# An adaLN attention block on one core: a new order for the first tasks, and the first 1/std replicated before the last scale group's products

## The chip, the cores and the metric

The kernel runs on one core of one Trainium2 chip. The metric is the device time of one execution in microseconds (us), the median over several runs. The profiled execution is one more run with the hardware profiler on; its span goes from the first to the last instruction of the program, and its own device time is a little longer than the span.

The engines: PE is TensorE (PEld its weight loads), DVE is VectorE, ACT is ScalarE, POOL is GpSimd, SP is SyncE, which here only issues transfers. Each works through its instructions in order.

## The reference

Two batches of 256 tokens, width D = 1152, all bf16:

```
mod = (silu(c) @ w_mod).reshape(B, 6, 1, D)
shift_a, scale_a, gate_a, ... = mod[:, 0], mod[:, 1], mod[:, 2], ...
h   = layernorm(x) * (1 + scale_a) + shift_a
qkv = h @ wqkv
p   = softmax(q @ k.T * D**-0.5)
out = x + gate_a * ((p @ v) @ wo)
```

## The kernel before

**Tiling.** The 512 tokens are four tiles of 128 (0 and 1 are batch 0, 2 and 3 batch 1). D is nine chunks of 128, called `cc` or `k`. Everything up to the attention is held transposed, with features on the partitions and tokens along the free axis, so `x` is transposed on PE first.

**The layer norm is split.** The mean is subtracted from the transposed x (`center`, L375). The chunk is then multiplied by `1 + scale` (`scale_x`, L470), which gives `h0T_sb`, stored in the tile `pvT_sb`. The division by the standard deviation is not done there. It is applied later, where scores and v leave PSUM, and for that 1/std and std are needed in two layouts: one value per token on the partitions (`rstd_sb`), and replicated over all partitions along the tokens (`rep_sb`, `std_sb`). `rep(b)` (L410) makes the second layout for batch b with two f32 transposes on PE from `lnv_sb`, the logarithm of the variance; `rep_out(b)` (L417) turns them into `rep_sb` and `std_sb` with two exponentials on ACT. `std_sb` is first read by `shift_x` (L482).

**The loads.** SP issues every weight load in the order of the list `LOADS`, into tiles written for the first time, so no load waits for compute. In it lie, among others, the four groups of scale columns of `w_mod` (`s` 0 to 3, covering chunks 0-1, 2-3, 4-5 and 6-8), between the row blocks of the key weights (`w`). Group 3 is issued after key rows 4-5 and before rows 6, 7 and 8.

**The front, an order written out by hand.** The list `ORDER` (L169 to L181) gives the order in which tasks of the first stage are emitted. Since each engine is in order, it fixes the order on each engine. The tasks:

- `('cT',)`, `('cTo',)`, `('e1',)`, `('d1',)`, `('rc',)`, `('scT',)`: c is transposed on PE, copied out by ACT, and silu(c) is made from it over ACT, POOL, DVE and POOL again.
- `('warm', 4)`: four products of zeros on PE, after five others (`warm(WARM)`).
- `('sum', i)`: row sums of x tile i on ACT (L387); `('nmT', i)` (L361) transposes and replicates such a mean into PSUM bank 6 on PE; `('mean', 3)` (L390) makes the mean of tile 3 with nine products by a matrix of ones.
- `('xT', i, part)` (L345): four or five PE transposes of x tile i into a PSUM bank; `('out', i, part, engine)` (L352) copies them to `xnT_sb`.
- `('nm', b, engine)` (L366) copies the replicated means of batch b from PSUM to `nm_sb`; `('cen', cc, tiles, engine)` centres a chunk, `('scale', cc, tiles, engine)` scales it.
- `('smm', g)` (L440) multiplies silu(c) by scale group g on PE, in bank 7, and `('sev', g)` (L447) reads the result on DVE and adds 1.
- `('early', k, ...)` and `('late', k)` are the key products of chunk k for the first five and the last two of seven key columns, each accumulating in its own bank (L491).
- `('sq', i)` (L397) makes the sum of squares on ACT.

**Behind the list** the code continues with the variance of batch 0 (`rstd_c(0)`, L405 and L407), centring and scaling of group 2, two more sums of squares, and then a loop over groups 2 and 3 (L585) that emits the key products of chunks 4 to 8. In chunk 5, after three of the seven columns, it emits `s_mm(3)` (L435), `scale_group(3)` and `rstd_c(1)`, and then goes on with the other four columns of chunk 5. `rep(0)` and `rep_out(0)` stand behind chunk 6, `rep(1)` and `rep_out(1)` behind chunk 7.

Then follow on PE: two more key columns, the shift products (`h_mm`), the query columns, v, scores, the gate, p @ v, and the product with `wo`. The dependence tracker (`_Prog`) turns reads and writes into semaphore waits; for a PSUM bank every access of another engine is waited for, whatever the columns.

Of the kernel before, what the change touches and what calls it, by code (L numbers as in the profile page):

```python
# [21 lines left out]
class _Prog:  # L22
# [12 lines left out]
    def op(self, eng, fn, r=(), w=(), dma=False, extra=()):  # L35
        o = _Op()
        o.eng, o.fn, o.dma = eng, fn, dma
        o.sem = o.val = None
        o.inc = False
        deps = set(extra)  # L40
        for k in r:
            if k[0] == "ps":
                continue
            p = self.last_w.get(k)
            if p is not None and not (p.eng == eng == PE):
                deps.add(p)
            self.readers.setdefault(k, []).append(o)
        for k in w:
            if k[0] == "ps":
                continue  # L50
            for q in self.readers.get(k, ()):
                if q is not o and (q.dma or dma or q.eng != eng):
                    deps.add(q)
            p = self.last_w.get(k)
            if p is not None and p is not o and not (p.eng == eng == PE):
                deps.add(p)
            self.readers[k] = [o] if k in r else []
            self.last_w[k] = o
        for k in set(r) | set(w):
            if k[0] != "ps":  # L60
                continue
            accesses = self.bank.setdefault(k, {})
            for e, q in accesses.items():
                if e != eng:
                    deps.add(q)
            accesses[eng] = o
        deps.discard(o)
        o.deps = deps
        self.ops.append(o)
        return o  # L70
# [73 lines left out]
D = 1152  # L144
# [21 lines left out]
CENTRED = (0, 1)  # L166
CUT = ("w", "qa", 8)
WARM = 5
ORDER = [  # L169
    ('sum', 2), ('cT',), ('xT', 2, 0), ('warm', 4), ('nmT', 2), ('cTo',), ('e1',), ('sum', 0), ('xT', 3, 0),  # L170
    ('xT', 3, 1), ('d1',), ('out', 3, 1, 'A'), ('out', 2, 0, 'D'), ('rc',), ('nmu2',), ('sum', 1), ('xT', 1, 0),
    ('xT', 2, 1), ('scT',), ('xT', 0, 0), ('out', 3, 0, 'D'), ('out', 1, 0, 'D'), ('mean', 3),
    ('out', 2, 1, 'D'), ('out', 0, 0, 'D'), ('xT', 1, 1), ('out', 1, 1, 'A'), ('smm', 0), ('nm', 1, 'D'),
    ('nmT', 0), ('nmT', 1), ('cen', 0, (2, 3), 'D'), ('sev', 0), ('xT', 0, 1), ('cen', 0, (0, 1), 'D'),
    ('nm', 0, 'D'), ('scale', 0, (2, 3), 'A'), ('scale', 0, (0, 1), 'A'), ('out', 0, 1, 'A'),
    ('cen', 1, (0, 1, 2, 3), 'D'), ('scale', 1, (2, 3), 'D'), ('early', 0, (2, 3)), ('early', 0, (0, 1)),
    ('sum', 3), ('scale', 1, (0, 1), 'D'), ('cen', 3, (0, 1, 2, 3), 'D'), ('late', 0), ('sq', 0), ('late', 1),
    ('smm', 1), ('cen', 2, (0, 1, 2, 3), 'D'), ('sev', 1), ('early', 1), ('scale', 2, (2, 3), 'D'),
    ('scale', 2, (0, 1), 'D'), ('scale', 3, (2, 3), 'D'), ('scale', 3, (0, 1), 'D'), ('late', 2), ('late', 3),
    ('early', 2), ('sq', 1), ('smm', 2), ('early', 3),  # L180
]  # L181


def bass_standalone__dit_adaln_block__diffusion_kernel(
    nc: bass.Bass,
    x: bass.AP,
    c: bass.AP,
    wqkv: bass.AP,
    wo: bass.AP,
    w_mod: bass.AP,  # L190
    out: bass.AP,
):
    with ExitStack() as es:
        _build(nc, es, x, c, wqkv, wo, w_mod, out)


def _build(nc, es, x, c, wqkv, wo, w_mod, out):
# [117 lines left out]
    for k0 in range(0, DC, 3):  # L315
# [7 lines left out]
        out=ident[:, :], in_=ident[:, :], compare_op=ALU.not_equal, fill=1.0,  # L323
# [78 lines left out]
    def rstd_c(b):  # L402
        i0, i1 = 2 * b, 2 * b + 2
        two = [("sq", i0), ("sq", i0 + 1)]
        op(AC, lambda a: a.activation(lnv_sb[:, i0:i1], sq_sb[:, i0:i1], ACT.Ln, bias=eps_sb[:, 0:1], scale=1.0 / D),  # L405
           r=two + [("eps",)], w=[("lnv", i0), ("lnv", i0 + 1)])
        op(AC, lambda a: a.activation(rstd_sb[:, i0:i1], lnv_sb[:, i0:i1], ACT.Exp, scale=-0.5),  # L407
           r=[("lnv", i0), ("lnv", i0 + 1)], w=[("rstd", i0), ("rstd", i0 + 1)])

    def rep(b):  # L410
        for i in (2 * b, 2 * b + 1):
            lo = NTOK + (i % 2) * P
            src = bass.AP(lnv_sb, i, [[TT, P], [0, P]])
            op(PE, lambda pe, src=src, lo=lo: pe.transpose(ps[7][:, lo:lo + P], src, ident32[:, :]),  # L414
               r=[("lnv", i), ("ident32",)], w=[("ps", 7)])

    def rep_out(b):  # L417
        lo, hi = b * NTOK, (b + 1) * NTOK
        for dst, sc, key in ((rep_sb, -0.5, "rep"), (std_sb, 0.5, "std")):
            op(AC, lambda a, dst=dst, sc=sc: a.activation(dst[:, lo:hi], ps[7][:, NTOK:2 * NTOK], ACT.Exp, scale=sc),  # L420
               r=[("ps", 7)], w=[(key, b)])
# [18 lines left out]
    def s_mm(g):  # L440
        a, b_ = SGROUPS[g]
        if g < SROWS:
            mod_mm(s_ap(g), [("ws", g)], a, b_, 0, a)
        else:
            rows_mm(s_off[g], b_ - a, [("ws", g)], ("mr", 0, a))
# [42 lines left out]
    def qk_mm(tag, src, key, col, k, bank, tiles=(0, 1, 2, 3), start=None):  # L488
        lo, hi = tiles[0] * P, (tiles[-1] + 1) * P
        rk = [(key, k, i) for i in tiles] if key == "h0" else [(key, k, b) for b in range(B)]  # L490
        op(PE, lambda pe: pe.matmul(ps[bank][:, lo:hi], wq_sb[:, k, col * P:(col + 1) * P],  # L491
                                    src[:, k, lo:hi], start=(k == 0) if start is None else start,
                                    stop=(k == DC - 1), skip_group_check=True),
           r=[("w", tag, k)] + rk, w=[("ps", bank)])
# [17 lines left out]
    early, late = tuple(range(EARLY)), tuple(range(EARLY, NA))  # L512
# [58 lines left out]
    def scale_group(g):  # L571
        s_ev(g)
        a, b_ = SGROUPS[g]
        for cc in range(a, b_):
            for b in range(B):
                scale_x(cc, (2 * b, 2 * b + 1), AC if b == 1 else DVE)
        if g + 1 < len(SGROUPS):
            center_group(g + 1)
# [6 lines left out]
    for g in range(2, len(SGROUPS)):  # L585
        a, b_ = SGROUPS[g]
        for k in range(a, b_):
            for j in range(NA):
                qk_mm("ka", h0T_sb, "h0", DC + j, k, j)
                if j == 2 and k == b_ - 1 and g + 1 < len(SGROUPS):  # L590
                    s_mm(g + 1)
                    scale_group(g + 1)
                    if g == 2:
                        rstd_c(1)
            b = k - 6
            if b in CENTRED:
                rep(b)
                rep_out(b)
    def shift_group(g):
        a, b_ = HGROUPS[g]  # L600
        for n, (cc, b) in enumerate((cc, b) for cc in range(a, b_) for b in range(B)):
            shift_x(cc, b)
# [172 lines left out]
    for i in range(TT):  # L775
        b = i // 2
# [65 lines left out]
```

## Time and profile before

| | us |
|---|---|
| median of 5 runs | 98.18 (97.81 to 98.42) |
| profiled execution, own time | 98.14 |
| its span | 96.4 |
| PE busy | 90.2 (94%) |
| DVE busy | 51.1 (53%) |
| ACT busy | 32.1 (33%) |
| POOL busy | 2.0 (2%) |

The page cuts the span into 40 slices of 2.41 us. Matmuls are pipelined: a record begins when a matmul starts to stream and lasts until its modelled end, so consecutive records overlap, and the distance from start to start is what one costs PE. A few matmul records are missing from the trace (697 matmuls against 705 weight loads). In a timeline line stand the start, the length, the engine, the line of the kernel, the operation, the output, the inputs, the shape and the number of instructions merged into that line; in square brackets, the idle time before it and what ended it.

### The profile page before, as it was taken

What the parts mean: (1) busy time and instruction counts of PE and PEld (TensorE: products, weight loads), DVE (VectorE), ACT (ScalarE), POOL (GpSimd) and SP (SyncE); (2) the same over time, 40 slices, a digit from 0 to 9 for tenths busy, and PEclk for the clock granted to TensorE, in tenths of its full rate; (3) what the DMA queues carried; (4) which work ended last, traced back from release to release, by engine and by line L of the source; (5) the groups of instructions that cost most, each with busy time, mean ns of one, the idle gap of its engine ahead of it and who ended that gap; (6) DMA issues with size and microseconds to landing.
All of it is one profiled execution on the core that took longest, in us unless ns stands there. A gap on an engine that the chain in (4) does not pass through costs nothing.

```text
span 96.4 us, 1728 instructions
## 1 busy us (share of the span) xinstructions
PE 90.2 (94%) x697; PEld 50.4 (52%) x705; DVE 51.1 (53%) x131; ACT 32.1 (33%) x65; POOL 2.0 (2%) x12
## 2 busy tenths in 40 slices
PE   5995899979999999999999999999999999999990
PEld 1475555435545454444444487454448866555670
DVE  1155994840367739404612075554307747499971
ACT  2696996956542200003220203336025700000000
POOL 5020000000000000000000000000000000000000
PEclk9999999999999999999999999999999999999999
DMA  2999999999999999999999992211477575712222
GB/s 22 373 310 346 333 314 346 358 315 340 366 368 366 379 336 361 388 394 392 391 391 391 392 293 33 46 31 27 22 27 45 46 46 48 126 55 82 82 82 82
DMA packets 20667, 22.03 MB, mean 229 GB/s; under 512 B 2610, under 2 KB 16690, under 8 KB 20660
## 3 DMA queue, kind: packets, MB, share of 16 engines
q1 hardware_dynamic: 20512, 21.63, 77.6%
q10 hardware_dynamic: 148, 0.30, 0.9%
q8 instruction: 5, 0.08, 0.3%
q14 instruction: 2, 0.02, 0.0%
HBM read 19.76 MB, written 1.18 MB: 217 GB/s over the span
## 4 chain that ended last, share of the span: by engine, by line
PE 74%; SPq 10%; DMA 9%; issue 1%; ACT 1%; DVE 1%
PE psbank L491 27%; PE psbank L785 18%; PE psbank L669 16%; DMA wm_sb<-in_w_mod_dram 9%; SPq L291 7%; PE psbank L747 4%; PE psbank L685 4%; PE psbank L656 2%; SPq L284 1%; PE psbank L435 1%; SPq L280 1%; PE psbank L726 1%; ACT qkT_sb L340 1%; ACT pvT_sb L480 1%; PE psbank L414 0%
## 5 line engine op out<-in xcount | busy, mean ns | idle before, releaser
L491 PE MATMUL psbank<-pvT_sb,wq_sb 128*128 128x512 bf16 (+1 forms) x82 | 18.1, 366 | 0.9 <-ACT pvT_sb L480 0.4
L491 PE MATMUL psbank<-hT_sb,wq_sb 128*128 128x512 bf16 x79 | 17.5, 379 | 0.2 <-issue 0.2
L785 PE MATMUL psbank<-wm_sb,pvT_sb 128*128 128x384 bf16 x99 | 16.3, 326 | 0.0
L669 PE MATMUL psbank<-wq_sb,hT_sb 128*128 128x512 bf16 x70 | 15.6, 379 | 0.2 <-issue 0.2
L785 PEld LDWEIGHTS psbank<-wm_sb,pvT_sb 128*128 128x128 bf16 x99 | 9.7, 98 | 6.3
L491 PEld LDWEIGHTS psbank<-hT_sb,wq_sb 128*128 128x128 bf16 x81 | 7.9, 98 | 9.4
L491 PEld LDWEIGHTS psbank<-pvT_sb,wq_sb 128*128 128x128 bf16 x86 | 7.7, 97 | 8.8 <-ACT pvT_sb L480 1.3
L340 ACT ACTIVATE qkT_sb<-psbank 128x512 bf16<-128x512 f32 x9 | 4.9, 603 | 19.5 <-PE psbank L491 19.5
L669 PEld LDWEIGHTS psbank<-wq_sb,hT_sb 128*128 128x128 bf16 x72 | 6.9, 98 | 8.3 <-DVE nb_sb L700 0.2
L338 DVE CAST qkT_sb<-psbank 128x512 bf16<-128x512 f32 x9 | 5.7, 683 | 9.5 <-PE psbank L491 9.5
L798 DVE TENSOR_TENSOR ga_sb<-psbank,gate_rep 128x384 bf16<-128x384 f32 x11 | 6.1, 553 | 3.2 <-PE psbank L785 3.0
L679 DVE TENSOR_SCALAR v_sb<-psbank,rstd_sb 128x512 bf16<-128x512 f32 x4 | 3.0, 749 | 8.8 <-PE psbank L669 8.8
L484 DVE SCALAR_TENSOR_TENSOR hT_sb<-std_sb,sh_sb,pvT_sb 128x256 bf16<-128x256 f32 x18 | 7.3, 478 | 0.1
L382 DVE TENSOR_TENSOR xnT_sb<-xnT_sb,nm_sb 128x512 bf16<-128x512 bf16 (+1 forms) x9 | 5.6, 655 | 0.1
L677 ACT ACTIVATE v_sb<-psbank,rstd_sb 128x512 bf16<-128x512 f32 x4 | 2.7, 683 | 7.3 <-PE psbank L669 7.3
L398 ACT ACTIVATE junk_sb<-x_sb,nmu_sb 128x1152 bf16<-128x1152 bf16 x4 | 5.0, 1251 | 0.1
L387 ACT ACTIVATE junk_sb<-x_sb 128x1152 bf16<-128x1152 bf16 x4 | 4.6, 1157 | 0.8 <-DMA x_sb<-in_x_dram 0.8
L332 PE MATMUL psbank<-warm_sb 128*128 128x512 bf16 x9 | 3.7, 563 | 1.2 <-DVE warm_sb L319 1.2
L702 ACT ACTIVATE e_sb<-s_sb,nb_sb 128x256 bf16<-128x256 bf16 x4 | 2.0, 508 | 8.2 <-DVE nb_sb L700 8.2
L801 DVE TENSOR_TENSOR xo_sb<-x_sb,ga_sb 128x384 bf16<-128x384 bf16 x11 | 3.9, 358 | 0.4
L480 ACT ACTIVATE pvT_sb<-xnT_sb,s_sb 128x256 bf16<-128x256 bf16 x7 | 3.2, 501 | 2.7 <-DVE s_sb L456 2.6
L747 PE MATMUL psbank<-pT_sb,v_sb 128*128 128x256 bf16 x36 | 4.1, 272 | 0.0
(72 smaller groups left out, 72.8 us busy)
## 6 DMA issues: line engine op xcount, KB each, us to landing
wq_sb<-in_wqkv_dram SPq DMA_DIRECT2D x3, 864.0 KB, 11.0
wm_sb<-in_w_mod_dram SPq DMA_DIRECT2D x1, 2592.0 KB, 16.1
wm_sb<-in_wo_dram SPq DMA_DIRECT2D x1, 2592.0 KB, 21.8
wq_sb<-in_wqkv_dram SPq DMA_DIRECT2D x4, 448.0 KB, 8.3
wm_sb<-in_w_mod_dram SPq DMA_DIRECT2D x3, 576.0 KB, 7.5
wm_sb<-in_w_mod_dram SPq DMA_DIRECT2D x1, 1440.0 KB, 10.5
wq_sb<-in_wqkv_dram SPq DMA_DIRECT2D x6, 224.0 KB, 7.2
wq_sb<-in_wqkv_dram SPq DMA_DIRECT2D x2, 576.0 KB, 10.4
```

What stands on the lines that cost most here:

```text
L291: op(SP, lambda e: e.dma_start(wq_sb[:, k0:k1, c0:c1], wq_v[:, k0:k1, c0:c1]), w=[("w", tag, k) for k in range(k0, k1)], dma=True)
L338: op(DVE, lambda v: v.tensor_copy(dst, src), r=r, w=w)
L340: op(AC, lambda a: a.activation(dst, src, ACT.Copy), r=r, w=w)
L382: op(eng, lambda e: e.tensor_tensor(ap, ap, nm, ALU.add), r=[("xnT", cc, i) for i in tiles] + nk, w=[("xnT", cc, i) for i in tiles])
L387: op(AC, lambda a: a.activation(junk_sb[:, :], x_sb[:, i, :], ACT.Copy, scale=sc, accum_out=dst[:, i:i + 1]), r=[("x", i)], w=[("junk", 0) ...
L398: op(AC, lambda a: a.activation(junk_sb[:, :], x_sb[:, i, :], ACT.Square, bias=nmu_sb[:, i:i + 1], scale=1.0, accum_out=sq_sb[:, i:i + 1]) ...
L484: op(DVE, lambda v: v.scalar_tensor_tensor(hT_sb[:, cc, lo:hi], std_sb[:, lo:hi], sh_sb[:, cc, b:b + 1], h0T_sb[:, cc, lo:hi], op0=ALU.mul ...
L491: op(PE, lambda pe: pe.matmul(ps[bank][:, lo:hi], wq_sb[:, k, col * P:(col + 1) * P], src[:, k, lo:hi], start=(k == 0) if start is None el ...
L669: op(PE, lambda pe, k=k, c0=c0, c1=c1, bank=bank: pe.matmul(ps[bank][:, 0:c1 - c0], hT_sb[:, k, i * P:(i + 1) * P], wq_sb[:, k, 2 * D + c0 ...
L747: op(PE, lambda pe, h=h, cc=cc, sbk=sbk: pe.matmul(ps[bank][:, h * NTOK:(h + 1) * NTOK], v_sb[:, 2 * b + sbk, cc * P:(cc + 1) * P], pT_sb[ ...
L785: op(PE, lambda pe, i=i, k=k, rhs=rhs, n=n, bank=bank: pe.matmul(ps[bank][:, 0:n], pvT_sb[:, k, i * P:(i + 1) * P], rhs, start=(k == 0), s ...
L798: op(DVE, lambda v, b=b, c0=c0, c1=c1, n=n, bank=bank, s=s: v.tensor_tensor(ga_sb[:, s, 0:n], ps[bank][:, 0:n], gate_rep[:, b, c0:c1], ALU ...
```

## The change

Two edits. The list `ORDER` is written in another order, and some of its tasks go to another engine. The loop behind it emits `rep(0)` and `rep_out(0)` ahead of chunk 6 where it emitted them behind chunk 6; `rep(1)` stays behind chunk 7.

On PE the task list now has all transposes of x, `mean` of tile 3 and the three `nmT` ahead of `s_mm(0)`; before, `nmT(0)`, `nmT(1)` and five transposes of tile 0 came behind it. `cT` and the warm-up products now stand ahead of the first transposes of x. From `s_mm(0)` to chunk 3 the order on PE is the same. On ACT, the copy of c's transposes stands ahead of the first row sum, and both `nm` copies come to it from DVE. Of the scalings, chunk 0 goes from ACT to DVE, and the batch 1 halves of chunks 1 and 2 go from DVE to ACT. The copy-out `('out', 3, 1)` goes from ACT to DVE. The number of instructions of each kind is the same but for these moves. SP's list of loads is untouched.

```
 ORDER = [
-    ('sum', 2), ('cT',), ('xT', 2, 0), ('warm', 4), ('nmT', 2), ('cTo',), ('e1',), ('sum', 0), ('xT', 3, 0),
-    ('xT', 3, 1), ('d1',), ('out', 3, 1, 'A'), ('out', 2, 0, 'D'), ('rc',), ('nmu2',), ('sum', 1), ('xT', 1, 0),
-    ('xT', 2, 1), ('scT',), ('xT', 0, 0), ('out', 3, 0, 'D'), ('out', 1, 0, 'D'), ('mean', 3),
-    ('out', 2, 1, 'D'), ('out', 0, 0, 'D'), ('xT', 1, 1), ('out', 1, 1, 'A'), ('smm', 0), ('nm', 1, 'D'),
-    ('nmT', 0), ('nmT', 1), ('cen', 0, (2, 3), 'D'), ('sev', 0), ('xT', 0, 1), ('cen', 0, (0, 1), 'D'),
-    ('nm', 0, 'D'), ('scale', 0, (2, 3), 'A'), ('scale', 0, (0, 1), 'A'), ('out', 0, 1, 'A'),
-    ('cen', 1, (0, 1, 2, 3), 'D'), ('scale', 1, (2, 3), 'D'), ('early', 0, (2, 3)), ('early', 0, (0, 1)),
-    ('sum', 3), ('scale', 1, (0, 1), 'D'), ('cen', 3, (0, 1, 2, 3), 'D'), ('late', 0), ('sq', 0), ('late', 1),
-    ('smm', 1), ('cen', 2, (0, 1, 2, 3), 'D'), ('sev', 1), ('early', 1), ('scale', 2, (2, 3), 'D'),
-    ('scale', 2, (0, 1), 'D'), ('scale', 3, (2, 3), 'D'), ('scale', 3, (0, 1), 'D'), ('late', 2), ('late', 3),
-    ('early', 2), ('sq', 1), ('smm', 2), ('early', 3),
+    ('cT',), ('warm', 4), ('cTo',), ('sum', 2), ('nmT', 2), ('e1',), ('xT', 2, 0), ('d1',), ('xT', 0, 0),
+    ('xT', 3, 0), ('rc',), ('xT', 3, 1), ('xT', 2, 1), ('sum', 0), ('nmT', 0), ('out', 2, 0, 'D'), ('nmu2',),
+    ('out', 3, 0, 'D'), ('scT',), ('sum', 1), ('xT', 1, 0), ('out', 3, 1, 'D'), ('mean', 3), ('out', 0, 0, 'D'),
+    ('out', 2, 1, 'D'), ('nm', 1, 'A'), ('xT', 0, 1), ('xT', 1, 1), ('nmT', 1), ('out', 1, 0, 'D'),
+    ('out', 1, 1, 'A'), ('cen', 0, (2, 3), 'D'), ('smm', 0), ('cen', 0, (0, 1), 'D'), ('nm', 0, 'A'),
+    ('out', 0, 1, 'A'), ('sev', 0), ('scale', 0, (2, 3), 'D'), ('early', 0, (2, 3)), ('scale', 0, (0, 1), 'D'),
+    ('cen', 1, (0, 1, 2, 3), 'D'), ('scale', 1, (0, 1), 'D'), ('cen', 3, (0, 1, 2, 3), 'D'),
+    ('cen', 2, (0, 1, 2, 3), 'D'), ('early', 0, (0, 1)), ('late', 0), ('scale', 1, (2, 3), 'A'), ('late', 1),
+    ('smm', 1), ('sev', 1), ('sum', 3), ('scale', 2, (2, 3), 'A'), ('scale', 2, (0, 1), 'D'), ('early', 1),
+    ('sq', 0), ('scale', 3, (0, 1), 'D'), ('late', 2), ('sq', 1), ('scale', 3, (2, 3), 'D'), ('late', 3),
+    ('early', 2), ('smm', 2), ('early', 3),
 ]
```

```
     for g in range(2, len(SGROUPS)):
         a, b_ = SGROUPS[g]
         for k in range(a, b_):
+            if k == 6:
+                rep(0)
+                rep_out(0)
             for j in range(NA):
                 qk_mm("ka", h0T_sb, "h0", DC + j, k, j)
                 if j == 2 and k == b_ - 1 and g + 1 < len(SGROUPS):
                     s_mm(g + 1)
                     scale_group(g + 1)
                     if g == 2:
                         rstd_c(1)
-            b = k - 6
-            if b in CENTRED:
-                rep(b)
-                rep_out(b)
+            if k == 7:
+                rep(1)
+                rep_out(1)
+
     def shift_group(g):
```

## The prediction

> **What bounds the kernel now.** I read the page first, then the chain of waits, then the timeline of the first 25 us, because everything that the change touches lies there.
>
> ```profile
> PE 90.2 (94%) x697; PEld 50.4 (52%) x705; DVE 51.1 (53%) x131; ACT 32.1 (33%) x65; POOL 2.0 (2%) x12
> PE   5995899979999999999999999999999999999990
> PEclk9999999999999999999999999999999999999999
> DMA  2999999999999999999999992211477575712222
> ```
>
> PE is full from the tenth slice on; the holes are in the first nine (up to 21.7 us). The transfers are full until 58 us. So two bounds are possible early: PE's own front, or the loads. The chain in order of time says which:
>
> ```profile
> 8.36 2.54 SPq L291
> 10.90 0.04 issue
> 10.94 9.03 DMA wm_sb<-in_w_mod_dram
> 19.97 0.04 issue
> 20.01 0.59 PE psbank L435 x36
> 20.61 0.02 issue
> 20.63 0.29 DVE sh_sb L453
> 20.93 0.02 issue
> 20.95 0.17 DVE s_sb L456
> 21.12 0.02 issue
> 21.14 0.52 ACT pvT_sb L480
> 21.66 0.04 issue
> 21.71 1.69 PE psbank L491 x7
> 23.39 0.22 PE psbank L414 x2
> 23.61 1.51 PE psbank L491 x7
> ```
>
> The reader is to see three stretches. Until 19.97 the chain is the load queue alone: the last of the four scale groups lands there, and nothing computed before is on the chain. From 20.01 to 21.71 it is one round trip: scale products on PE, two steps on DVE, one scaling on ACT. From 21.71 it is PE without a hole worth naming, to 94.03 of 96.4. So a microsecond saved before 19.97 counts only if the load comes sooner too, and one saved on PE after 21.71 counts in full. The timeline around the landing gives the slack on both sides:
>
> ```profile
> 16.48 3.18 PE L491 MATMUL psbank<-pvT_sb,wq_sb 128*128 128x512 bf16 x14
> 20.01 0.57 PE L435 MATMUL psbank<-wm_sb,scT_sb 128*32 128x96 bf16 x36 [0.35 <-DMA wm_sb<-in_w_mod_dram]
> 20.51 0.55 PEld L491 LDWEIGHTS psbank<-pvT_sb,wq_sb 128*128 128x128 bf16 x4
> 20.74 0.81 PE L491 MATMUL psbank<-pvT_sb,wq_sb 128*128 128x512 bf16 x3 [0.16 <-DMA wq_sb<-in_wqkv_dram]
> 21.71 1.69 PE L491 MATMUL psbank<-pvT_sb,wq_sb 128*128 128x512 bf16 x7 [0.16 <-ACT pvT_sb L480]
> ```
>
> PE stood 0.35 us before the landing by modelled ends. A wide matmul occupies its slot for (1.69 - 0.38) / 6 = 0.218 us, where 0.38 is the length of a single record there; so the slot before had been free for about 0.35 + 0.38 - 0.22 = 0.5 us. That is PE's slack at the landing.
>
> **The change, part by part.**
>
> *rep(0) moved ahead of chunk 6.* Two f32 transposes leave the stream behind chunk 6: 0.22 us, from the chain (23.39 to 23.61), on the path. They come back behind the last four products of chunk 5. Four weight loads but three matmul records stand there, so one record is missing: the four start at 20.74 and every 0.213 to 0.218 us after it, and the last slot ends at about 21.60. Chunk 6 started at 21.71, when ACT's scaling (21.14 + 0.52 = 21.66) released it. The empty slot is 0.11 us. The transposes take it and 0.11 us more, so chunk 6 starts at 21.82 and ends 0.11 us later, but nothing of 0.22 us follows it. Sum: -0.22 + 0.11 = **-0.11 us**. Bounds: 0, if the gap is only the pipeline's drain and the transposes push chunk 6 by their whole 0.22; -0.22, if both fit, as by the modelled ends (20.74 + 0.81 = 21.55, then 0.16 idle) they nearly do. I take -0.11, from starts rather than modelled ends.
>
> Their inputs aren't late. `lnv` of batch 0 is written at 15.33 + 0.29 = 15.62. Bank 7 was last read by DVE's L453, done at 20.92; both precede 21.60. Two exponentials on ACT go with them: 0.38 us each, in the same place of ACT's order, behind the variance of batch 1 (22.67 + 0.20). They now find PE done and run at 22.87 instead of 23.65. `rep(1)` must wait for them in bank 7: they end at about 23.53, it comes at 24.9. The first reader of `std_sb` starts at 29.82. No cost.
>
> *The new front.* What does it do to the start of the key products (10.33), and then to 20.01? By queue, with durations from this trace:
>
> - ACT: copy of c's transposes at 3.87 (they end on PE at 3.84) for 0.17; the first sum at 4.05 instead of 3.79, since one such sum goes every 1.16; e1 at 5.21 (5.15 before); the next sums at 5.36 and, behind another accumulation (1.38 apart, as the squares at 12.57 and 13.95), at 6.74, done at about 8.0.
> - PE: with the warm-up 0.4 us earlier it waits for the first sum until 5.31 + 0.06 and then does 22 transposes at (1.51 - 0.27) / 21 = 0.06 us, one `nmT` (0.11), four transposes, nine mean products (0.06 each): 7.9. `nm(1)`, now on ACT, waits for these and the sum: 8.1 to 8.5 (0.38 as L420's, 0.42 as DVE's before). Behind it wait `nmT(1)` and with it all of PE, to about 8.65.
> - The first scale products were held by their load: they began at 8.94 after 1.01 us idle. PE is ready at 8.65, so they still begin at 8.94.
> - DVE: `sev(0)` at 9.57 as before. Then the scaling of chunk 0 is a DVE step of 0.24 (0.48 for two) where ACT took 0.52, so the key products start at about 10.05 instead of 10.33.
>
> DVE's added work is hidden: the 640-wide copy-out taken from ACT, 0.48 at most, is followed by three copies of 0.38 from start to start, the last done by 8.5, ahead of 8.94. It gives up two 0.42 `nm` copies. ACT, with two `nm` more, still frees itself in time: scaling of chunk 1 at about 10.9, sum 3 to 12.5, scaling of chunk 2 at 12.94, squares from 13.34 to 16.1 (2.76 for both and their readout), variance to 16.62. Its next step, scaling chunk 4, began at 16.64 before. POOL keeps its order but for nothing: d1 at 5.5, `scT` at about 6.1, needed at 8.94.
>
> So the front gains up to 0.28 us. Worth at the end: **0 us**, hidden by the 0.5 us wait for the load, which only gets longer. Bounds: 0.28 gained in full if the load were no bound; and lost, if the new order were late by L, then max(0, L - 0.5). My sum has the one new wait, `nmT(1)` behind ACT's `nm(1)`, 0.29 us ahead of the load. An error of one 1.16 us sum there makes L = 1.16 - 0.29 - 0.28 = 0.6, a loss of 0.1. These are the ends: -0.28 and +0.1.
>
> *Loads.* SP's queue doesn't change, nothing in it waits for compute before 36 us, and ACT's two early issues stand first as before. 0. Later landings leave room for a PE that is 0.1 us early: the first shift group was issued at 15.55 and took 11.7, so 27.3 against its use at 28.72; the second 22.54 + 10.5 = 33.0 against 34.41.
>
> One rule speaks against the change. The Trainium skill, TensorE: Matmul & The Clock Gate, section Part 4: PE-mode transpose, says that transposes don't count as activity for the clock the way matmuls do, and the change puts 41 x-transposes in one run. In this trace the granted clock is 1.00 in every window from 3.4 to 28 us, and behind 37 transposes of x the ten half-width and four wide key products from 10.33 took 2.17 us with a wait of 0.33 in it, the full pace, so the row disagrees with the fear. By the rule, half speed would add some 1.9 us to those fourteen, 1.4 beyond the slack, an estimate of 99.4; by the row nothing, and I go by the row.
>
> **Sum.** -0.11 + 0 + 0 against the profiled execution's 98.14 (span 96.4 and 1.74 around it) gives 98.03. The median is 98.18, so the profiled run stands 0.04 below it; I say **98.03 us**. What a measurement here can tell from no change is about 0.5%, 0.49 us. The forecast is within it.
>
> **Rivals.**
>
> 1. *The load isn't the bound in most runs.* The five times spread over 0.6 us. If the scale group lands 0.5 us earlier in typical runs, PE is the bound at 19.5, and the front's 0.28 counts: 98.14 - 0.11 - 0.28 = 97.75; with every small wait gone (the 0.33 at 11.89 too) 97.4, past -0.5%. For: the spread. Against: the chain shows loads alone up to 19.97. Chance 0.22, most of it still within 0.5%.
> 2. *Slower: ACT is the late one at 21.14.* Chunk 6 needs ACT free when DVE hands over at 21.12. Before, its last square was read out at 19.97 + 0.19 = 20.16, a margin of 0.98. It now carries the `nm` copies and the scalings of chunks 1 and 2 ahead of all four squares. It decides once ACT is over 0.98 us later than before, and each microsecond beyond costs one. If both squares of batch 0 slip by one sum more (1.16) and the own-engine waits (0.22 each) come on the four squares, ACT is 2.0 late and the kernel 1.0 - 0.11 = 0.9 slower: 99.0. Against: my sum has it free at 16.62 for a 16.64 start. Chance 0.10.
> 3. *The move does nothing.* The transposes push chunk 6 by all of 0.22, and the load hides the front: 98.14. For: after each of the small-row products PE shows a drain of 0.14 to 0.16. Against: here it is ACT's end at 21.66 that releases. Chance 0.18.
>
> **How the numbers follow.** Forecast 0.50, rivals 0.22, 0.10 and 0.18. Forecast and rival 3 lie within 0.5%; of rival 1 about 0.13 is beyond -0.5% with 0.09 within; rival 2 is beyond +0.5% save 0.01. So faster 0.13, same 0.78, slower 0.09. The range: low 97.55, rival 1 at its better half, high 98.55, rival 3 with the upper part of the spread of the runs (98.42) and a front that loses 0.1; outside lie the worst of rival 2 and the best of rival 1.
>
> **What would show it.** Right: the scale products of L435 again begin near 20.0 after an idle time that a load ends, longer than 0.35; L414 stands once between 21.5 and 21.9 and once near 24.9; the seven products after the first follow without it; key products begin near 10.05. Wrong: idle time of PE at L435 that ends on ACT or DVE, or none; L480 at chunk 6 behind L398; L491 at 10 us with starts 0.2 us apart for half width; a first key product later than 10.9.

## The result and the profile after

The changed kernel takes 97.93 us (median of 54 runs, 97.38 to 98.64) against 98.14 for the kernel before (94 runs, 97.61 to 99.42). The ratio is 0.9975, with a 95% interval from 0.9964 to 0.9986: 0.24 us faster, between 0.14 and 0.35. The forecast was 98.03, 0.11 us faster. The profiled execution took 97.67 with a span of 95.9. Medians here are over all runs; the ratios leave out runs more than 1.5% above the fastest of the same kernel.

The chain of waits of the changed kernel, in order of time (start, length, what), cut to the early part of the program (`...` marks pieces left out):

```profile
2.12 7.00 DMA wm_sb<-in_w_mod_dram
9.12 0.14 issue
9.25 0.60 PE psbank L426 x18
...
10.08 0.48 DVE pvT_sb L476 x2
10.56 0.61 DVE xnT_sb L382
...
11.19 0.52 ACT pvT_sb L480
...
19.76 0.57 PE psbank L435 x36
20.32 0.16 issue
20.48 0.81 PE psbank L491 x3
21.29 0.22 PE psbank L414 x2
21.51 3.13 PE psbank L491 x14
24.65 0.22 PE psbank L414 x2
```

Two things have changed. The chain no longer waits for the last scale group's load up to 19.97: it goes through the first scale group's load, landed at 9.12, and then through the engines. And behind L435 the round trip over DVE and ACT is gone from it: the first pair of L414 stands where the chain went through ACT, and 14 products of chunks 6 and 7 follow without it.

The timeline of the same stretch (start, length, engine, line, operation, tiles, shape, count, idle time before and what ended it):

```profile
19.76 0.42 PEld L435 LDWEIGHTS psbank<-wm_sb,scT_sb 128*32 128x32 bf16 x36 [0.52 <-DMA wm_sb<-in_w_mod_dram]
20.48 0.81 PE L491 MATMUL psbank<-pvT_sb,wq_sb 128*128 128x512 bf16 x3 [0.16 <-issue]
20.89 1.31 ACT L480 ACTIVATE pvT_sb<-xnT_sb,s_sb 128x256 bf16<-128x256 bf16 x3 [0.55 <-DVE s_sb L456]
21.13 0.38 PE L414 MATMUL psbank<-ident,lnv_sb 128*128 128x128 f32 x2
21.45 3.19 PE L491 MATMUL psbank<-pvT_sb,wq_sb 128*128 128x512 bf16 x14
21.45 2.70 PEld L491 LDWEIGHTS psbank<-pvT_sb,wq_sb 128*128 128x128 bf16 x14 [0.18 <-ACT pvT_sb L480]
```

From the start of L435 to the first product of chunk 6 it is 21.45 - 19.76 = 1.69 us, against 21.71 - 20.01 = 1.70 before. So the two transposes now stand in this round trip and did not lengthen it at all. The last line shows that ACT's scaling still releases chunk 6: its weight load sat idle 0.18 us for it. The chain is drawn by modelled ends, which is why it goes through the transposes there.

The times of the two profiled spans can't simply be subtracted, though. L435 itself began 0.25 us earlier in this execution (19.76 against 20.01), and the experiments show how much that start moves from one execution to the next. What can be compared to 0.01 us is the distance from L435 to the product with `wo`, the last long piece of each chain. Before and after:

```profile
76.45 17.59 PE psbank L785 x117
```

```profile
75.97 17.59 PE psbank L788 x117
```

76.45 - 20.01 = 56.44 us before, 75.97 - 19.76 = 56.21 after: 0.23 us less, with what remains of the span behind it unchanged but for rounding.

### The profile page after: what moved, and what is told of

Read it like the earlier page. It is cut to its first block, busy times and chain, and to the rows that moved or that the text cites. A ratio compares the mean times of both kernels' runs of the same rounds, so it can differ in the third digit from the quotient of the medians.

```text
span 95.9 us, 1730 instructions
## 1 busy us (share of the span) xinstructions
PE 90.2 (94%) x697; PEld 50.4 (53%) x705; DVE 50.7 (53%) x130; ACT 32.0 (33%) x66; POOL 1.9 (2%) x12
## 3 DMA queue, kind: packets, MB, share of 16 engines
HBM read 19.76 MB, written 1.18 MB: 218 GB/s over the span
## 4 chain that ended last, share of the span: by engine, by line
PE 84%; DMA 7%; DVE 2%; issue 1%; SPq 1%; ACT 1%
PE psbank L491 35%; PE psbank L788 18%; PE psbank L672 16%; DMA wm_sb<-in_w_mod_dram 7%; PE psbank L688 4%; PE psbank L750 4%; PE psbank L659 2%; PE psbank L426 2%; PE psbank L435 1%; SPq L280 1%; PE psbank L729 1%; DVE xnT_sb L382 1%; ACT qkT_sb L340 1%; ACT pvT_sb L480 1%; DVE pvT_sb L476 1%
## 5 line engine op out<-in xcount | busy, mean ns | idle before, releaser
L688 PE MATMUL psbank<-qkT_sb 128*128 128x256 bf16 x36 | 4.1, 272 | 0.0
```

The source lines that it names most:

```text
L688: op(PE, lambda pe, cc=cc: pe.matmul(ps[bank][:, 0:NTOK], qkT_sb[:, cc, i * P:(i + 1) * P], qkT_sb[:, DC + cc, b * NTOK:(b + 1) * NTOK], s ...
```

## The experiments

The theory at this point, A: the replication's move is worth its whole 0.22 us, and the new task order nothing. Its rivals were B (0.11 for the move, as predicted, and the rest for the order) and C (all of it the order). Ratios are to runs of the kernel before beside them, each with its 95% interval; every kernel has one trace, of one execution; "tail" is the distance from L435 to the product with `wo`.

### Each half of the change alone

The move of the replication, with the old task order:

```
+            if k == 6:
+                rep(0)
+                rep_out(0)
...
-            if b in CENTRED:
-                rep(b)
-                rep_out(b)
+            if k == 7:
+                rep(1)
+                rep_out(1)
```

> The old task order, with only the replication of batch 0 moved ahead of chunk 6. Theory A (the two transposes fit wholly into the empty slot before chunk 6, and the task order is hidden by the load of the last scale group): -0.22 us, 97.9 against 98.14, all of the change's gain; L414 first stands between 21.3 and 21.6 and chunk 6 starts 1.70 us after L435, as before. Theory B (the slot is 0.11 wide as predicted, the task order gives the rest): -0.11 us, chunk 6 starts 1.8 us after L435. Theory C (all of the gain is the task order): 0.

Measured: 98.02 against 98.07, ratio 0.9981 (0.9951 to 1.0011). That alone tells A from neither rival. The trace does:

```profile
16.22 1.02 PE L491 MATMUL psbank<-pvT_sb,wq_sb 128*128 128x512 bf16 x4
18.14 2.32 PE L491 MATMUL psbank<-pvT_sb,wq_sb 128*128 128x512 bf16 x10 [0.89 <-DMA wq_sb<-in_wqkv_dram]
20.57 0.57 PE L435 MATMUL psbank<-wm_sb,scT_sb 128*32 128x96 bf16 x36
21.95 0.38 PE L414 MATMUL psbank<-ident,lnv_sb 128*128 128x128 f32 x2
22.27 1.04 PE L491 MATMUL psbank<-pvT_sb,wq_sb 128*128 128x512 bf16 x4
```

Chunk 6 starts 22.27 - 20.57 = 1.70 us after L435, with the two transposes between. The tail is 76.79 - 20.57 = 56.22, as in the changed kernel. This execution is nevertheless 0.3 us longer than the profiled one of before (span 96.7), and the second line says why: the key weights of chunk 4 came 0.89 us late, and the last scale group after them. The move does what A says; what made this execution long is the loads, ahead of L435.

The new task order, with the old place of the replication:

```
 ORDER = [
-    ('sum', 2), ('cT',), ('xT', 2, 0), ('warm', 4), ('nmT', 2), ('cTo',), ('e1',), ('sum', 0), ('xT', 3, 0),
...
+    ('cT',), ('warm', 4), ('cTo',), ('sum', 2), ('nmT', 2), ('e1',), ('xT', 2, 0), ('d1',), ('xT', 0, 0),
...
```

> The new task order, with the replication left behind chunk 6. Theory A: 0 us within 0.1, and L435 waits for its load as before. Theory B: -0.13 us. Theory C: -0.25 us, with L435 starting earlier by as much in every run.

Measured: 98.19 against 98.07, ratio 1.0006 (0.9975 to 1.0038). The tail is 76.17 - 19.73 = 56.44, that of the kernel before. So nothing behind L435 comes from the order. With the run before, in which the move alone shortens the tail by 0.22, C falls. The chain of this run does not begin with the scale group's load. It begins with the last tile of x:

```profile
1.66 5.75 DMA x_sb<-in_x_dram
7.44 0.04 issue
7.49 1.26 ACT junk_sb L387 x2
8.74 0.28 ACT nm_sb L373
9.02 0.04 issue
9.07 0.32 PE psbank L363
9.39 0.56 PE psbank L426 x18
```

Tile 1 of x landed at about 7.4. Its row sum, ACT's `nm(1)` behind it and the transpose of the mean then held PE until the first scale products at 9.35, and the load of those products was there before.

### How much room is in front of L435

Four products of zeros, 256 wide, put on PE ahead of the third scale products:

```
         elif n == "smm":
+            if args[0] == 2:
+                for _ in range(4):
+                    op(PE, lambda pe: pe.matmul(ps[7][:, 256:512], warm_sb[:, 0:P], warm_sb[:, 0:256],
+                                                start=True, stop=True), r=[("warm",)], w=[("ps", 7)])
             s_mm(*args)
```

In the kernel before:

> The kernel before, with four more products of zeros (256 wide, 0.107 us each, 0.43 in all) on PE ahead of the third scale products. Theory A (PE waits some 0.5 us in free slots for the last scale group): hidden, 0 to +0.1 us. Rival (in typical runs the load comes sooner than in the profiled one and PE is the bound): +0.43 us.

Measured: 98.15 against 98.07, ratio 1.0020 (0.9990 to 1.0050). In the changed kernel:

> The changed kernel, with the same four products of zeros (0.43 us) ahead of the third scale products. Theory A with a front that gained: hidden, 0 to +0.05 against the changed kernel, so -0.2 against the kernel before. Rival (PE is the bound at the last scale products): +0.43 against the changed kernel, +0.2 against the kernel before.

Measured: 98.19 against 98.08, ratio 1.0017 (0.9985 to 1.0050), which is 0.41 us above the changed kernel's own 0.9975. By the middle values the 0.43 us that were put in were paid about in full there, and about half in the kernel before; but each interval is about 0.3 us either way, and that of the kernel before reaches from nothing to the whole 0.43. In both traces PE was the bound at L435, no longer the load:

```profile
20.17 0.42 PEld L435 LDWEIGHTS psbank<-wm_sb,scT_sb 128*32 128x32 bf16 x36 [0.42 <-issue]
```

```profile
20.52 0.42 PEld L435 LDWEIGHTS psbank<-wm_sb,scT_sb 128*32 128x32 bf16 x36 [0.42 <-issue]
```

These two lines, of the kernel before and of the changed kernel with the four products, also show how to read the idle time in front of L435. Even where nothing is waited for, the weight load of these narrow products stands 0.42 us after the end of the one before it. Only what exceeds 0.42 is a wait for the load. In the profiled run of before the same line is

```profile
20.01 0.42 PEld L435 LDWEIGHTS psbank<-wm_sb,scT_sb 128*32 128x32 bf16 x36 [0.85 <-DMA wm_sb<-in_w_mod_dram]
```

so the wait is 0.85 - 0.42 = 0.43 there, and 0.52 - 0.42 = 0.10 in that of after.

The other direction takes 224 KB out of the queue ahead of the last scale group, with the old and with the new order. The key weights of chunk 5 are not loaded, and chunk 5 is multiplied by those of chunk 4: the keys come out as other ones, while the work of the engines stays the same.

```
-    ('x', 0), ('x', 1), ('s', 0), ('w', 0, 1), ('w', 1, 2), ('s', 1), ('w', 2, 4), ('s', 2), ('w', 4, 6),
+    ('x', 0), ('x', 1), ('s', 0), ('w', 0, 1), ('w', 1, 2), ('s', 1), ('w', 2, 4), ('s', 2), ('w', 4, 5),
...
+        kw = 4 if tag == "ka" and k == 5 else k
...
```

> The kernel before, with the rows of key weights of chunk 5 not loaded; chunk 5 is multiplied by those of chunk 4, so the keys are other ones and the work on the engines is the same. That takes 224 KB, some 0.67 us at 340 GB/s, out of the queue ahead of the last scale group. Theory A (that load is the bound): faster by the 0.5 us of free slots, until PE is the bound: -0.4 to -0.5 us. Rival (the load is not the bound): 0.

Measured: 97.71 against 98.08, ratio 0.9965 (0.9939 to 0.9991), 0.34 us faster (0.09 to 0.60). The loads were a bound in typical executions; whether by more or less than the 0.5 us of the prediction, this interval can't tell. In the trace L435 starts at 19.82 behind a bare 0.42; from the second scale products at 12.56 that is 7.26 us. No trace shows less than 7.25, so I take this as PE's own work between the two.

> The same cut in the load with the new task order and the old place of the replication. If the front gained the 0.28 us that the prediction worked out, and the last scale group's load hid it, it shows here: -0.2 to -0.28 us against the run with the cut and the old order. If the front's gain was already lost at the load of the second scale group (which ended PE's wait at 12.40 in the changed kernel's trace) the two are equal within 0.1.

Measured: 97.79 against 98.08, ratio 0.9968 (0.9937 to 1.0000): no gain over the same cut with the old order that these runs could show, to about 0.3 us either way. In the two traces L435 starts 0.17 us earlier with the new order (19.65 against 19.82). The groups at the first two scale products, of the old order with the cut and then of the new one, show what the order does:

```profile
9.17 0.59 PE L426 MATMUL psbank<-scT_sb,wm_sb 128*128 128x2 bf16 x18 [0.51 <-DMA wm_sb<-in_w_mod_dram]
10.55 2.18 PE L492 MATMUL psbank<-pvT_sb,wq_sb 128*128 128x256 bf16 x13 [0.24 <-ACT pvT_sb L480]
12.56 0.59 PE L426 MATMUL psbank<-scT_sb,wm_sb 128*128 128x2 bf16 x18
```

```profile
9.14 0.59 PE L426 MATMUL psbank<-scT_sb,wm_sb 128*128 128x2 bf16 x18 [0.15 <-DMA wm_sb<-in_w_mod_dram]
10.30 2.13 PE L492 MATMUL psbank<-pvT_sb,wq_sb 128*128 128x256 bf16 x13 [0.58 <-DVE pvT_sb L476]
12.38 0.52 PEld L426 LDWEIGHTS psbank<-scT_sb,wm_sb 128*128 128x128 bf16 x18 [0.45 <-DMA wm_sb<-in_w_mod_dram]
```

From scale products to key products it is 1.38 us with the old order and 1.16 with the new: 0.22 gained, by chunk 0's scaling on DVE. At the second scale products PE then meets their load, and the new order waits there: from the key products to them (12.39 on PE itself) it is 12.39 - 10.30 = 2.09 us, where 1.96 is enough in the two other traces of this order without a wait for that load (10.52 to 12.48 with the order alone, 10.79 to 12.75 in the version below). So 0.13 of the gain goes there.

### Both replications in the round trip

If theory A is right, the round trip still had room: 0.32 us (worked out under "Why the prediction was right" below), of which 0.22 were used. The next version fills it with the replication of batch 1 too, in the free half of bank 7:

```
             if k == 6:
                 rep(0)
+                rep(1)
                 rep_out(0)
+                rep_out(1)
...
                     s_mm(g + 1)
+                    if g == 2:
+                        ln_c(1)
                     scale_group(g + 1)
```

Here `ln_c(b)` is the logarithm (L405) alone, which leaves `rstd_c(b)` with the exponential, and `rep(1)` with its `rep_out` uses columns 0 to 255 of the bank; the old place behind chunk 7 is empty. With the new order:

> The changed kernel, with the logarithm of batch 1 put ahead of the last scalings on ACT and the replication of batch 1 put ahead of chunk 6 too, beside that of batch 0. Four transposes, 0.44 us, then stand where the empty slot is 0.32 by theory A: chunk 6 starts 0.12 later and nothing of 0.22 follows behind chunk 7: -0.10 us against the changed kernel, -0.35 against the kernel before. By theory B (slot 0.11, already overfilled): chunk 6 is 0.22 later, 0 against the changed kernel.

Measured: 97.76 against 98.07, ratio 0.9966 (0.9937 to 0.9994). Chunk 6 now starts 21.81 - 20.00 = 1.81 us after L435, 0.11 later than before, and the tail is 76.11 - 20.00 = 56.11, another 0.10 shorter. That is A's arithmetic to 0.02 us. B, in which the gap was overfilled already, falls.

With the old order, only `ORDER` put back:

> The old task order, with the replications of both batches ahead of chunk 6 and the logarithm of batch 1 ahead of the last scalings. Theory A (the order is worth nothing over many runs, the replications are worth 0.22 + 0.10): -0.32 us against the kernel before, the same as with the new order. Theory D (the new order is a loss, since its first scale products wait for the last x tile to land: they began at 9.14 to 9.61 in the traces with it and at 8.68 to 9.17 in those with the old one): -0.4 to -0.5 us. If the order is a gain: -0.2 us or less.

Measured: 98.37 against 98.23, ratio 0.9995 (0.9958 to 1.0032). The tail is 75.66 - 19.56 = 56.10, the same gain, and the profiled execution the shortest of all at 97.36. Its twelve runs are spread from there to 99.22, and the interval goes from -0.41 to +0.31 us. It holds the -0.32 of A near its edge, and also a gain of less than 0.2, the expectation if the new order is a gain. So its times decide nothing about the order. Its timeline has the record that is missing elsewhere (only this trace and the next run's have it):

```profile
19.56 0.57 PE L438 MATMUL psbank<-wm_sb,scT_sb 128*32 128x96 bf16 x36
20.06 1.04 PE L494 MATMUL psbank<-pvT_sb,wq_sb 128*128 128x512 bf16 x4
20.93 0.60 PE L417 MATMUL psbank<-ident,lnv_sb 128*128 128x128 f32 x4
21.37 4.48 PE L494 MATMUL psbank<-pvT_sb,wq_sb 128*128 128x512 bf16 x20
```

Here all four products of chunk 5 are recorded (line numbers are three higher). They begin at 20.06, 0.50 after L435's start, without the 0.16 us of idle time that the other traces show, and the transposes come at 20.93, exactly 4 x 0.218 us later. So the missing record is the first of the four, not the last. In the next run's trace it is the same: 20.56 behind 20.06.

At last, the new order with both replications, and the first scale products moved ahead of the transpose of the last mean; on DVE the scale's readout and the scaling of batch 1's half go ahead of the centring of batch 0's half:

```
-    ('out', 2, 1, 'D'), ('nm', 1, 'A'), ('xT', 0, 1), ('xT', 1, 1), ('nmT', 1), ('out', 1, 0, 'D'),
-    ('out', 1, 1, 'A'), ('cen', 0, (2, 3), 'D'), ('smm', 0), ('cen', 0, (0, 1), 'D'), ('nm', 0, 'A'),
-    ('out', 0, 1, 'A'), ('sev', 0), ('scale', 0, (2, 3), 'D'), ('early', 0, (2, 3)), ('scale', 0, (0, 1), 'D'),
+    ('out', 2, 1, 'D'), ('nm', 1, 'A'), ('xT', 0, 1), ('xT', 1, 1), ('smm', 0), ('nmT', 1), ('out', 1, 0, 'D'),
+    ('out', 1, 1, 'A'), ('cen', 0, (2, 3), 'D'), ('sev', 0), ('scale', 0, (2, 3), 'D'), ('cen', 0, (0, 1), 'D'), ('nm', 0, 'A'),
+    ('out', 0, 1, 'A'), ('early', 0, (2, 3)), ('scale', 0, (0, 1), 'D'),
```

> The new order and both replications ahead of chunk 6, with the first scale products moved ahead of the transpose of the last mean, and on DVE the scale's readout and the scaling of batch 1's half ahead of the centring of batch 0's half. Theory D: the first scale products start when their load lands, not behind the last x tile's mean; 0 to -0.2 us against the same kernel without this move, where PE is the bound at the last scale products. Theory A: the load of the last scale group bounds it, 0 against the same.

Measured: 98.00 against 98.23, ratio 0.9994 (0.9963 to 1.0025). The first scale products started on their load again (9.00), but the second ones came at 12.62, no earlier than with the old order: between them PE's weight loads sat idle 0.56 us for ACT's scaling, behind ACT's copy-out. L435 came at 20.06, behind its load. The tail is 76.17 - 20.06 = 56.11. No gain from this move can be seen.

### The table that decides

Starts from the profiled execution of each kernel. "First" and "second" are the starts of the first and the second scale products.

| kernel | order | first | second | L435 | `wo` | tail |
|---|---|---|---|---|---|---|
| before | old | 8.94 | 12.34 | 20.01 | 76.45 | 56.44 |
| order alone | new | 9.35 | 12.48 | 19.73 | 76.17 | 56.44 |
| before, four products of zeros | old | 9.08 | 12.48 | 20.17 | 76.60 | 56.43 |
| before, less loaded | old | 9.17 | 12.56 | 19.82 | 76.25 | 56.43 |
| order alone, less loaded | new | 9.14 | 12.39 | 19.65 | 76.08 | 56.43 |
| after | new | 9.25 | 12.40 | 19.76 | 75.97 | 56.21 |
| replication alone | old | 8.68 | 12.08 | 20.57 | 76.79 | 56.22 |
| after, four products of zeros | new | 9.57 | 12.82 | 20.52 | 76.73 | 56.21 |
| both replications | new | 9.61 | 12.75 | 20.00 | 76.11 | 56.11 |
| both replications | old | 8.71 | 12.27 | 19.56 | 75.66 | 56.10 |
| both, scale products first | new | 9.00 | 12.62 | 20.06 | 76.17 | 56.11 |

The tail takes three values, to 0.01 us, and only the place of the replications decides which. Where L435 stands has no such order: without the products of zeros and the cut load it lies from 19.56 to 20.57 with the old task order and from 19.73 to 20.06 with the new one.

The first two columns show what became of the new front. Where their load delays the second scale products by 0.02 us at most, they start 3.13 to 3.15 us after the first ones with the new order (order alone, after, both replications) and 3.39 to 3.40 with the old one (before, its versions with zeros and with less loaded, replication alone). That is a gain of 0.25 us. But the first scale products start at 9.14 to 9.61 with the new order as the prediction had it, and at 8.68 to 9.17 with the old one, and so the second ones are no earlier. In two traces of the new order they start on their own load (9.25 and 9.14), in the other three (9.35, 9.57 and 9.61) behind work that had waited 0.6 to 1.0 us for a tile of x. How much of this is the order, which wants the means of all four tiles ahead of them where the old one wanted those of tiles 2 and 3, and how much is when the loads happened to land, one trace for each kernel doesn't show.

## Why the prediction was right, and where it was not

**The sign and the main term.** The forecast was that the moved replication gives the gain and the new front gives nothing that counts. The tail shows 0.23 us of gain, the whole kernel 0.24 (0.14 to 0.35); what is left for the order is 0.0 with about 0.1 us either way. The order alone measured 1.0006 (0.9975 to 1.0038), in agreement. The nearness of 98.03 to 97.93 says little by itself: the forecast's 0.11 us lies outside the measured 0.14 to 0.35, and the times of two of the three rivals, 97.75 and 98.14, lie within the stated range too.

**The mis-sized term: "The empty slot is 0.11 us", hence -0.11.** It measured 0.32 us, and the term -0.22, the prediction's own upper bound. The step that failed is the place of the missing record. Three of four products were recorded from 20.74 on, and the prediction took the fourth to stand behind them, ending at 21.60. It stands ahead of them, from about 20.51 on, where the 0.16 us looked like idle time, so the four slots end at 20.74 + 3 x 0.218 = 21.39 and 21.71 - 21.39 = 0.32 us were free. The version with both replications, 0.11 over the slot with 0.44 us in it, gives the same: 0.44 - 0.11 = 0.33.

**The front.** Right in its worth, 0, as far as these runs can tell, and right that chunk 0's scaling on DVE brings the key products closer: 0.22 us closer to the scale products, by the two runs with the cut load, where the prediction had 0.28; from the first to the second scale products it is 0.25. Two parts of the reason did not hold. One is "PE is ready at 8.65": it assumed x where the trace of before had it. In the run with the order alone x came later, and PE was ready only at 9.35. The new wait that the prediction named, the last mean's transpose behind ACT's `nm(1)`, is then the bound, and the cause is a transfer that its bounds did not contain, not a row sum too many. The other is that the last scale group's load hides the gain behind 0.5 us. In the profiled run of before that wait was 0.41 to 0.43; in that of after 0.10; with the order alone 0. By the distance of 7.26 us from the second scale products, PE was the bound there in several executions. So what cancels the front's gain in these traces is mainly the later start of the first scale products, 9.25 in the changed kernel where the prediction kept 8.94; at the second scale group's load 0.13 us went with the order alone and less loaded, but only 0.02 in the changed kernel. That it comes to nothing is thus partly luck: the reason given, the wait at the last scale group, was nearly gone or not there.

**The signs.** The key products begin at 10.42, not near 10.05. At L435 the line of PE shows no idle time, which the prediction had named as a sign of being wrong; only the weight load's line still ends on the load, with 0.10 us beyond its usual 0.42. L414 stands at 21.13 and 24.48, earlier than both places named. That the seven products behind chunk 6 follow without it came true.

**The loads.** SP's list was indeed unaffected, and no later load turned into a wait: the tails would not agree to 0.01 us otherwise. What the prediction treated as a fixed landing time differs between the traces, and all that varies between traces with the same place of the replications lies ahead of L435.

**The rivals.** The first, PE as the bound at L435, came true in several traces, without its price, since the front's gain was lost ahead of it. The second, ACT late at chunk 6, did not come: the last square was read out at 20.16 + 0.19 = 20.35, and ACT then sat idle 0.55 us until DVE handed over, where before it was 0.98. ACT was 0.19 us later than before rather than level: its scaling of chunk 2 waited for DVE's readout of the second scale group until 13.23, where the prediction had 12.94, and from there none of its rows up to 20.35 shows idle time. The third, the move without effect, is excluded by the tail. Its argument, a drain of 0.14 to 0.16 us behind the small-row products, does not hold at L435: where all four records are there, the next product starts 0.50 us after L435 without idle time.

**The clock.** The rule that transposes don't count as activity (The Trainium skill, TensorE: Matmul & The Clock Gate, Part 4: PE-mode transpose) cost nothing here. The granted clock of the profiled execution was 1.00, and the fourteen key products behind the transposes went from 10.42 to 12.40, 1.98 us; by the 0.218 us of a wide one and half of it for a half-width one they need 10 x 0.109 + 4 x 0.218 = 1.96. The traces have 36 transposes of x, before and after, not the 37 and 41 that the prediction counts.

**What stays open.** Whether the new order is worth something between -0.1 and +0.1 us can't be told from these runs. Nor does the version with both replications stand as measured faster than the changed kernel: its tail is 0.10 us shorter in three traces, but the ratios of the three kernels are 0.9966, 0.9995 and 0.9994, each with an interval of about 0.003 either way, and the spread of the load stage covers the difference.

## What to carry to other kernels

Where a stage that varies from run to run stands ahead of one that does not, measure from a fixed point behind it: here the same distance, taken in different traces, agrees to 0.01 us while the times of the same kernel spread over 1 us. Small independent work belongs into the round trip that an engine waits out, and the room there is counted from slots of one instruction each, with the missing records put in their place; compare weight loads with matmuls, and look for an idle time that is too regular. And an order that does more work ahead of a product can start it no earlier than the last transfer which this work needs.

## What the runs showed of the hardware

The start of L435, which the weight loads and the front set between them, moved by 1.0 us between profiled executions of different versions (19.56 to 20.57) although SP's list was the same. In one of them (replication alone) PE sat idle 0.89 us for the key rows of chunk 4; no other trace shows this wait.

The weight load of the 32-column products begins 0.42 us after the end of the weight load before it, even where no wait is shown. It was so at L435 in both runs with products of zeros, and ahead of the first shift products of the kernel before and of the changed kernel, whose line this is:

```profile
28.25 0.51 PEld L435 LDWEIGHTS psbank<-wm_sb,scT_sb 128*32 128x32 bf16 x36 [0.42 <-issue]
```

An f32 transpose of 128x128 costs PE 0.11 us from start to start: 0.22 for two behind a chunk (24.48 to 24.70 in the changed kernel), 0.44 for four (20.93 to 21.37 with the old order and both replications).
